# Five more filler matmuls around and within the wide part of an output projection

## The chip, the cores and the metric

The kernel runs on one core of one Trainium2 chip. The metric is the device time of one execution in microseconds; lower is better. Two numbers belong to an execution: the device time, and the span of its instructions on the core, which is 1.4 to 2.0 us shorter. Positions in the traces are counted from the start of the span.

## The reference

The reference mixes two branches with a scalar gate. Branch A is one decode step of attention over long caches; branch B is a gated MLP over a sequence of one. Only A's end matters here.

```python
def reference(A_x, A_k_cache, A_v_cache, A_wq, A_wo, B_x, ..., gate_w):
    g = sigmoid((A_x * gate_w).sum(-1, keepdims=True))
    # A: H = 32 heads, Sk = 16384 keys, Dh = 128, D = 512
    q = (A_x @ A_wq).reshape(...)                     # [1, 32, 1, 128]
    p = softmax(einsum('bhqd,bhkd->bhqk', q, A_k_cache) * Dh ** -0.5)
    o = einsum('bhqk,bhkd->bhqd', p, A_v_cache)
    a = o.reshape(1, 1, 32 * 128) @ A_wo              # output projection, A_wo [4096, 512]
    b = ...                                           # small, done at the start
    return g * a + (1 - g) * b                        # [1, 1, 512]
```

Each cache is 134 MB of bf16. The kernel reads 279.58 MB in all and does little arithmetic for each byte.

## The kernel before

K and V stream through three SBUF buffers. Of the output weights, `wo` has 32 rows for each partition; they are loaded last, in pieces. The projection has two parts. The *wide* part takes rows 0 to 23 in three rounds of eight matmuls with one output row each, in the column groups at 0, 32, 64 and 96 in turn. Their partial sums are copied out by ScalarE (`d_sb`) and folded in with one more product. The *narrow* part takes rows 24 to 31 as they land, two matmuls of 256 columns for each row, in the column groups at 0 and 32.

```python
WO_CUTS = (0, 16, 24, 28, 31, 32)   # pieces of the load, in rows
WIDE, WG = 24, 8

def warm(e, n):              # n fillers: full 128-column matmuls of zeros
    for j in range(n):
        args = (m_ps[0], ident[:, :], zero[:, :])
        ...                  # the first loads its weights, the others don't

def fill(e, m, n=1):         # n fillers of m weight columns (so m output rows), in the column group at 96
    for _ in range(n):
        matmul_again(nc, e, m_ps[0][96:96 + m, :], ident[:, 0:m], zero[:, :], start=True,
                     stop=True, skip_group_check=True)
...
pe.raw(lambda e: warm(e, 2))
t_ok = pe.op(lambda e: e.transpose(oT_ps, o_sb[:, :], ident[:, :]), ...)
...
pe.raw(lambda e: warm(e, 1))
# 4 small matmuls that spread the heads' outputs into o2
...
def pe_wide(e):
    va, pa = (counter(e, n, 0) for n in ("wa", "oa"))
    warm(e, 2)
    with e.Fori(0, WIDE // WG) as t:
        ...                  # 8 matmuls into d_ps, column groups 0, 32, 64, 96 in turn
        registers_first(nc, n, lambda: take(e, wo_s))      # waits for this round's weights
        ins.then_inc(pe.sem, 1)
        fill(e, 1)
        ...
w_ok = act.op(lambda e: e.copy(out=d_sb[:, :], in_=d_ps), wait=[(pe.sem, pe.n)], mark=True)
...
for j, (a, b) in enumerate(zip(WO_CUTS[:-1], WO_CUTS[1:])):
    for k in range(max(a, WIDE), b):                       # narrow part
        y_ok = add(o2[:, k:k + 1], wo[:, k * D:(k + 1) * D],
                   [(ld_o[j], 16)] if k == a else (), k == H - 1)
    if b == 28:
        add(ones_f[:, 0:1], d_sb[:, :], [w_ok])            # folds the wide sums in
# then two copies to res (VectorE, ScalarE) and the store
```

The outputs of `warm` and `fill` are never read.

The softmax here doesn't subtract the row's maximum and nothing guards it: scores larger than these inputs give would overflow.

## Time and profile before

| | before |
|---|---|
| median of the first 3 executions | 651.94 us (651.72 to 652.34) |
| span of the profiled execution | 650.2 us |
| data read | 279.58 MB, 430 GB/s |
| PE / VectorE busy | 65% / 52% of the span |
| load of rows 24 to 27, which the narrow part awaits first, landed | 646.88 us |
| last PE step (20 narrow matmuls) | 1.64 us |

Lines of the profile's page of the kernel before: the span, the busy times, the DMA share in 40 slices (tenths of a slice), and the load queue's share of the 16 DMA engines:

```profile
span 650.2 us, 7735 instructions
PE 423.0 (65%) x2464; PEld 44.4 (7%) x1304; DVE 336.0 (52%) x159; ACT 45.8 (7%) x112; POOL 2.1 (0%) x10
...
DMA  9999989999999999999999989999999999999898
...
q1 hardware_dynamic: 6194, 279.58, 99.6%
```

The loads run from beginning to end; no engine comes near that. Next the end of the chain of waits of the kernel before (start, length, what):

```profile
619.38 27.50 DMA bufs<-in_A_wo_dram
...
646.92 1.64 PE ps_all L716 x20
...
648.58 0.41 DVE res L731
```

The chain names one load of weights, that of rows 24 to 27; then come 1.64 us of narrow matmuls and the copies. A second wait is hidden in that step: the loads of rows 28 to 31 land later, and the last eight narrow matmuls wait for them (their weight loads for 0.47 us, until 647.91). The timeline of PE over the same stretch of the kernel before (start, length, line, what; in brackets the idle time ahead of it). L91 is a filler (the first filler of a `warm` stands under L477), L106 is here a wide round, L716 is the narrow part:

```profile
642.42 0.38 PE L91 MATMUL ps_all<-zero,ident 128*128 128x512 bf16 x1
643.33 0.60 PE L106 MATMUL ps_all<-bufs,o 128*1 x8 [0.54 <-PEq L86]
643.77 0.38 PE L91 MATMUL ps_all<-zero,ident 128*1 128x512 bf16 x1
644.24 0.60 PE L106 MATMUL ps_all<-bufs,o 128*1 x8
...
645.80 0.60 PE L106 MATMUL ps_all<-bufs,o 128*1 x8 [0.73 <-PEq L86]
646.24 0.38 PE L91 MATMUL ps_all<-zero,ident 128*1 128x512 bf16 x1
646.92 0.60 PE L716 MATMUL ps_all<-bufs,o 128*1 128x256 bf16 x8 [0.31 <-DMA bufs<-in_A_wo_dram]
647.36 0.60 PE L716 MATMUL ps_all<-d_sb,const-float32-1.0 128*1 128x256 f32 x4
647.91 0.60 PE L716 MATMUL ps_all<-bufs,o 128*1 128x256 bf16 x8
```

The third wide round waits 0.73 us to be handed its weights, and the narrow part 0.31 us for its load. The fillers lie in between.

Their purpose is the clock. The windows view of the kernel before (stretch; its length; busy time and count for PE, weight loads, VectorE, ScalarE, POOL; then granted PE clock, DMA share, GB/s) shows it at 0.50 after an idle stretch (PE idled from 629.0 to 631.0) and back at 1.00 in the microsecond from 635, and shows it at 1.00 where the narrow part runs (from 646.92 on):

```profile
630.00:631.00 1.00, 0.00 (x0) 0.00 (x0) 0.00 (x0) 0.00 (x0) 0.00 (x0) 1.00 1.04 442
...
632.00:633.00 1.00, 1.00 (x13) 0.31 (x14) 0.00 (x0) 0.00 (x0) 0.00 (x0) 0.50 0.89 377
...
635.00:636.00 1.00, 1.00 (x16) 0.28 (x10) 0.00 (x0) 0.00 (x0) 0.00 (x0) 1.00 1.08 451
...
646.00:647.00 1.00, 0.69 (x11) 0.08 (x4) 0.00 (x0) 0.55 (x1) 0.00 (x0) 1.00 1.02 396
647.00:648.00 1.00, 1.00 (x14) 0.44 (x15) 0.00 (x0) 0.04 (x1) 0.00 (x0) 1.00 0.44 143
```

### The profile page before, as it was taken

The numbers are of one execution on the slowest core, as the hardware profiler recorded it, in microseconds if no ns is written. First come the engines' busy times: TensorE is split into PE (matmuls) and PEld (weight loads), VectorE is DVE, ScalarE is ACT, GpSimd is POOL, SyncE is SP. The second block draws the span as 40 slices with busy tenths as digits, with TensorE's granted clock in tenths as the row PEclk, the third lists the DMA queues.
The fourth block names the chain that finished last, engine by engine and source line by source line (L and its number), as shares of the span: only waits on it lengthen the run. The fifth ranks groups of instructions, "written<-read, shape, count | busy, mean of one in ns | idle before, by whom it ended". The sixth has DMA issues, their size and how long they took to land. (4 is left out here: it accounts for less than half of the span.)

```text
span 650.2 us, 7735 instructions
## 1 busy us (share of the span) xinstructions
PE 423.0 (65%) x2464; PEld 44.4 (7%) x1304; DVE 336.0 (52%) x159; ACT 45.8 (7%) x112; POOL 2.1 (0%) x10
## 2 busy tenths in 40 slices
PE   0547587847387574747857476584747757478767
PEld 0000000000101000010000101000010100001012
DVE  3457848256380845618265370835629075465600
ACT  2200100000001000010100001000010100001011
POOL 1000000000000000000000000000000000000000
PEclk9959788969779696987969798686978968798999
DMA  9999989999999999999999989999999999999898
GB/s 385 462 419 452 452 387 452 452 439 399 452 452 399 439 452 448 391 452 452 407 431 452 452 387 452 452 423 415 452 452 391 448 452 448 391 431 472 390 432 341
DMA packets 6203, 279.60 MB, mean 430 GB/s; under 512 B 695, under 2 KB 826, under 8 KB 1210
## 3 DMA queue, kind: packets, MB, share of 16 engines
q1 hardware_dynamic: 6194, 279.58, 99.6%
q8 instruction: 1, 0.02, 0.0%
q10 hardware_dynamic: 8, 0.00, 0.0%
HBM read 279.58 MB, written 0.00 MB: 430 GB/s over the span
## 5 line engine op out<-in xcount | busy, mean ns | idle before, releaser
L579 DVE TENSOR_TENSOR bufs<-bufs,qb x64 | 281.5, 4419 | 170.8 <-DVEq L86 170.8
L91 PE MATMUL ps_all<-bufs,ident 128*128 x960 | 261.6, 427 | 0.0
L496 PE MATMUL ps_all<-bufs,ident 128*128 x64 | 28.4, 444 | 153.8 <-PEq L86 153.8
L106 PE MATMUL ps_all<-bufs,p_t 128*8 x1024 | 79.2, 385 | 30.7 <-PEq L86 20.1
L564 DVE TENSOR_REDUCE s_sb<-ps_all 128x64 f32<-128x512 f32 x64 | 44.1, 688 | 95.0 <-DVEq L86 95.0
L91 PE MATMUL ps_all<-zero,ident 128*8 128x512 bf16 (+1 forms) x165 | 58.0, 383 | 0.0
L592 ACT ACTIVATE p_t<-s_sb 64x256 f32 (+1 forms) x32 | 13.3, 414 | 433.4 <-ACTq L86 433.0
L496 PEld LDWEIGHTS ps_all<-bufs,ident 128*128 128x128 bf16 x64 | 6.3, 99 | 367.7 <-issue 367.7
L106 PEld LDWEIGHTS ps_all<-bufs,p_t 128*8 x1024 | 17.9, 82 | 163.7 <-issue 163.5
L531 PE MATMUL ps_all<-pick,d_sb 128*128 128x2 f32 x128 | 16.9, 254 | 16.5 <-PEq L86 16.5
L531 PEld LDWEIGHTS ps_all<-pick,d_sb 128*128 128x128 f32 x128 | 15.7, 192 | 34.7 <-issue 34.7
L601 ACT COPY d_sb<-ps_all 128x512 f32<-128x512 f32 x16 | 9.4, 586 | 104.5 <-ACTq L86 104.5
L606 ACT CAST ps_all<-zero 128x512 f32<-128x512 bf16 x15 | 8.8, 589 | 1.7
L666 DVE RECIPROCAL rl<-ps_all 128x32 f32<-128x32 f32 x1 | 0.4, 357 | 11.3 <-PE ps_all L552 11.3
L669 DVE TENSOR_TENSOR o_sb<-ps_all,rl 128x32 bf16<-128x32 f32 x1 | 0.2, 192 | 11.5 <-PE ps_all L531 11.5
L592 ACT ACTIVATION_READ_ACCUMULATOR p_t<-s_sb (+1 forms) x32 | 5.9, 185 | 0.0
L381 DVE TENSOR_TENSOR bufs<-ps_all,ident 128x896 f32<-128x896 f32 x2 | 2.1, 1086 | 7.3 <-PE ps_all L91 7.3
L321 PE MATMUL ps_all<-xgw,const-float32-1.0 1*128 1x3 f32 x2 | 0.6, 360 | 8.0 <-DVE xgw L317 8.0
L106 PE MATMUL ps_all<-bufs,u 128*1 x14 | 2.6, 372 | 3.3 <-ACT ps_all L427 2.5
L91 PE MATMUL ps_all<-bufs,xb 128*128 x12 | 4.1, 467 | 0.0
L345 PE MATMUL ps_all<-bufs,xb 128*128 x4 | 1.9, 485 | 3.1 <-DMA bufs<-in_B_w_in_dram 3.1
L297 PE MATMUL ps_all<-const-bfloat16-1.0,x_row 1*128 1x128 bf16 x4 | 0.6, 302 | 4.8 <-DMA x_row<-in_A_x_dram 4.8
(76 smaller groups left out, 41.2 us busy)
## 6 DMA issues: line engine op xcount, KB each, us to landing
bufs<-in_A_k_cache_dram SPq DMA_DIRECT2D x2, 4096.0 KB, 35.7
bufs<-in_A_v_cache_dram SPq DMA_DIRECT2D x1, 5120.0 KB, 34.0
bufs<-in_A_wq_dram SPq DMA_DIRECT2D x1, 4096.0 KB, 12.3
bufs<-in_A_v_cache_dram SPq DMA_DIRECT2D x1, 2048.0 KB, 38.6
bufs<-in_A_wo_dram SPq DMA_DIRECT2D x1, 2048.0 KB, 24.6
bufs<-in_B_w_in_dram SPq DMA_DIRECT2D x1, 1792.0 KB, 15.5
bufs<-in_A_v_cache_dram SPq DMA_DIRECT2D x1, 1024.0 KB, 40.6
bufs<-in_A_wo_dram SPq DMA_DIRECT2D x1, 1024.0 KB, 26.7
```

The source lines that it names most:

```text
L91: ins = eng.matmul(out, lhsT=lhsT, rhs=rhs, **flags).ins
L106: ins = eng.matmul(bank[0:m, 0:n], lhsT=lhsT, rhs=rhs, **flags).ins
L297: x_ok = pe.op(lambda e, c=c: e.matmul(m_ps[1][:, c * P:(c + 1) * P], lhsT=x_row[0:1, c::DC], rhs=ones_row[0:1, :], start=True, stop=True) ...
L345: if n else matmul_on(nc, e, lambda: e.matmul(args[0], lhsT=args[1], rhs=args[2], **flags), [at, (xa, 0)]))
L381: dve.op(lambda e, h=h, zh=zh: e.tensor_tensor(out=zm[:, 2 * h * ZB:2 * (h + 1) * ZB].rearrange("p (b m k) -> p b m k", b=2, k=FhC), in0=z ...
L496: matmul_on(nc, e, lambda: e.matmul(s3, lhsT=ident[:, :], rhs=k3[:, :, 0:W], start=True, **flags), [(kw, 0)])
L531: ins = e.matmul(o2, lhsT=d_sb[:, r * Dh:(r + 1) * Dh], rhs=pick[:, r * 2:(r + 1) * 2], start=False, stop=False, skip_group_check=True)
L564: return e.tensor_reduce(out=s_sb[:, c * QK:(c + 1) * QK], in_=s_ps[c % 2].rearrange("p (j w) -> p j w", w=W), axis=AX.X, op=ALU.add)
L579: e.tensor_tensor(out=k3, in0=k3, in1=qi, op=ALU.mult).then_inc(mul_s, 1)
L592: e.activation(out=p_t[rows, bass.ds(at, NG * 8)].rearrange("p (t c) -> p t c", c=8)[:, :, 4 * s:4 * s + 4], in_=s_sb[rows, :].rearrange(" ...
L601: return e.copy(out=d_sb[:, :], in_=d_ps)
L606: e.copy(out=d_ps, in_=zero[:, :]).then_inc(drn_s, 1)
```

## The change

The change aims to keep PE busier, and so its clock up, through the end of the kernel; with no filler in the tail, in a run below, the clock stayed at 0.50 from 642.6 us to the end. It adds one filler ahead of the wide rounds, one in each of the three rounds, and one between the last round and the narrow part: five executed matmuls.

```diff
     def pe_wide(e):
         va, pa = (counter(e, n, 0) for n in ("wa", "oa"))
-        warm(e, 2)
+        warm(e, 3)
         with e.Fori(0, WIDE // WG) as t:
             ...
             ins.then_inc(pe.sem, 1)
-            fill(e, 1)
+            fill(e, 1, 2)
             ...
+    pe.raw(lambda e: fill(e, 1))
     for j, (a, b) in enumerate(zip(WO_CUTS[:-1], WO_CUTS[1:])):
         for k in range(max(a, WIDE), b):
             y_ok = add(o2[:, k:k + 1], wo[:, k * D:(k + 1) * D],
```

## The prediction

> **What bounds the kernel now.** The DMA queue. The page's slices show DMA at 9 almost everywhere: 279.58 MB in 650.2 us, packets on 99.6% of the 16 engines' span. PE is busy 65%, DVE 52%. The chain of waits that ended last is, for 27.50 us, one load of output weights (issued at 619.38, landed at 646.88), then 1.64 us of PE (20 narrow matmuls), 0.41 us of DVE copy, and the store.
>
> The tail, from the timeline: fillers at 642.19 and 642.42; wide groups at 643.33, 644.24 and 645.80, each 8 matmuls (0.60 us) and one filler; narrow part at 646.92 (waits for a load), 647.36, and 647.91 (waits for another). Group 3 sits idle 0.73 us before its weights are handed over. So loads pace the tail at three places, and the fillers lie between them.
>
> **What the change does.** It removes and moves nothing. It adds five executed filler matmuls of zeros into an unread region of PSUM: one before the wide loop, one in each of its 3 rounds, one after it. A row of three fillers takes 0.81 us, one 0.38: (0.81 - 0.38)/2 = 0.215 us of array time each, 1.1 us in all. The intent must be the clock: [...] after PE idled from 629.0 to 631.0 the windows view shows 0.50 from 632 to 634 and 1.00 after 635.
>
> **How much is on the critical path.**
> - Before the loop: array free at about 642.64, group 1 at 643.33; 0.215 of 0.69 us is used.
> - Rounds 1 and 2: the period is 0.91 us; group 2 may slip by up to 0.1 us, but group 3 waits for a load until 645.8, which takes that up.
> - Round 3 and after: the filler at 646.24 is followed by two, at about 646.46 and 646.67; the last one's slot ends at about 646.89, the narrow part started at 646.92. They just fit. Slip 0 to 0.1 us, absorbed before 647.91, where the last loads gate again.
>
> Gain: in the profiled run the windows view shows clock 1.00 in every microsecond from 638 to 650, so nothing is to be gained there. If some executions have a cold tail, the narrow part runs at half speed in those, partly hidden behind the loads: estimated from its 1.64 us, 0.3 to 1.6 us. The three timed runs differ by 0.62 us, which leaves room for a few tenths on the median.
>
> **Prediction: 651.85 us, range 651.1 to 652.6.** Faster by over 2%: 0.005; within 2%: 0.99; slower by over 2%: 0.005. If anything, 0.1 us faster.
>
> **What would show it right.** The last chain is still one load of output weights of about 27.5 us, then about 1.64 us of PE; clock 1.00 in the tail; two fillers per wide round and one more before and after.
>
> **What would show it wrong.** The narrow part starting later than its load landed (fillers in the way); a longer last PE step, or narrow matmuls over 300 ns (clock). A change before 642 us cannot follow from this edit.
>
> **What would make it wrong.** A cold tail in most timed runs of before, though not in the profiled one (gain up to 1.6 us); fillers [...] delaying the last matmuls (loss of 0.2 to 0.4 us); chip-to-chip differences in load speed, which would move both kernels.

## The result, and the profile after

| | before | after |
|---|---|---|
| median, first comparison (6 executions each) | 651.78 us (651.63 to 652.34) | 651.65 us (651.61 to 652.38) |
| span of the profiled execution | 650.2 us | 650.3 us |
| third wide round to start of the narrow part | 1.12 us | 1.13 us |
| start of the narrow part to the copies | 1.66 us | 1.65 us |

The ratio is 0.9999, 95% interval 0.9986 to 1.0012: the same. Ratios here and below are the mean time of one kernel's fast executions over that of the other's in the same rounds, so not quite the ratio of the medians quoted.

The page of the kernel after:

```profile
span 650.3 us, 7740 instructions
PE 423.2 (65%) x2469; PEld 44.6 (7%) x1304; DVE 335.9 (52%) x159; ACT 45.8 (7%) x112; POOL 2.1 (0%) x10
```

There are exactly five more PE instructions. The timeline of PE in the kernel after:

```profile
642.57 0.59 PE L91 MATMUL ps_all<-zero,ident 128*128 128x512 bf16 x2
643.47 0.60 PE L106 MATMUL ps_all<-bufs,o 128*1 x8 [0.31 <-PEq L86]
643.91 0.59 PE L91 MATMUL ps_all<-zero,ident 128*1 128x512 bf16 x2
644.38 0.60 PE L106 MATMUL ps_all<-bufs,o 128*1 x8
...
645.95 0.60 PE L106 MATMUL ps_all<-bufs,o 128*1 x8 [0.53 <-PEq L86]
646.38 0.81 PE L91 MATMUL ps_all<-zero,ident 128*1 128x512 bf16 x3
647.08 0.60 PE L716 MATMUL ps_all<-bufs,o 128*1 128x256 bf16 x8
...
648.06 0.60 PE L716 MATMUL ps_all<-bufs,o 128*1 128x256 bf16 x8
```

Everything stands about 0.15 us later than in the trace of before. This shift is there already ahead of the first edited instruction (the small matmul on L677 starts at 642.15 instead of 642.00), so the edit did not cause it. Relative to each other the steps kept their places: the two rounds are still 0.91 us apart, and the narrow part follows the third round by 1.13 us. The idle times became fillers: 0.73 us ahead of the third round is now 0.53, and the 0.31 us ahead of the narrow part are gone. Yet the narrow part starts no sooner. Its wait is still in the trace, on the weight loads, which have no filler ahead of them. First the waits view of before, then that of after (who waited for whom: total us, times, longest):

```profile
PEld ps_all L716 <- DMA bufs<-in_A_wo_dram: 1.5, 2, 1.0
...
PE ps_all L716 <- DMA bufs<-in_A_wo_dram: 0.3, 1, 0.3
```

```profile
PEld ps_all L716 <- DMA bufs<-in_A_wo_dram: 1.5, 2, 1.0
```

The clock is full here too, where the narrow part runs (windows view of the kernel after):

```profile
647.00:648.00 1.00, 1.00 (x13) 0.44 (x12) 0.00 (x0) 0.18 (x1) 0.00 (x0) 1.00 0.52 176
```

The chain of waits of the kernel after looks very different, though nothing moved:

```profile
645.95 0.60 PE ps_all L106 x8
646.55 0.65 PE ps_all L91 x3
647.20 1.51 PE ps_all L716 x20
...
648.73 0.41 DVE res L732
```

It no longer goes back to the load, because PE has no gap left there. A filled gap is not a removed wait: the chain now calls PE the limit, and the experiments below say that it is not.

### The profile page after: what moved, and what is told of

Same layout as the page of the kernel before. It is cut to its first block, busy times and chain, and to the rows that moved or that the text cites. A ratio compares the mean times of both kernels' runs of the same rounds, so it can differ in the third digit from the quotient of the medians.

```text
span 650.3 us, 7740 instructions
## 1 busy us (share of the span) xinstructions
PE 423.2 (65%) x2469; PEld 44.6 (7%) x1304; DVE 335.9 (52%) x159; ACT 45.8 (7%) x112; POOL 2.1 (0%) x10
## 5 line engine op out<-in xcount | busy, mean ns | idle before, releaser
L91 PE MATMUL ps_all<-zero,ident 128*8 128x512 bf16 (+2 forms) x170 | 59.0, 382 | 0.0
L106 PE MATMUL ps_all<-bufs,xb 128*64 x32 | 3.6, 381 | 0.0
```

The source lines that it names most:

```text
L91: ins = eng.matmul(out, lhsT=lhsT, rhs=rhs, **flags).ins
L106: ins = eng.matmul(bank[0:m, 0:n], lhsT=lhsT, rhs=rhs, **flags).ins
```

## The experiments

Theory A: in most executions the clock is full at the end anyway, the loads pace it, and the five fillers lie in slack, so nothing is gained or lost. Rival B: some executions of before end with a cold clock, which the fillers cure, so there is a gain hidden in the spread. A second question is what a filler costs once it no longer fits in slack.

### The changed kernel again (no edit)

> The changed kernel once more, unaltered, with more rounds. Theory A (the clock was already full and the loads gate the tail, so the fillers lie in slack): 651.7 us, within 0.05% of before, clock 1.00 from 638 to 650. Rival B (some executions of before have a cold tail which the fillers cure): before shows more executions of 0.5 us or longer above its lowest than this kernel does, and the mean is 0.1 to 0.3 us lower.

Measured: 651.62 us median of 5 (651.53 to 651.86) against 651.84 for 9 executions of before (651.59 to 652.11); ratio 0.9997, interval 0.9984 to 1.0011. The means differ by 0.17 us in the direction of rival B, and 1 of 9 executions of before against 0 of 5 lies 0.5 us or more above the lowest; neither is clear of noise. The expected clock was wrong, and usefully so: in steps of 0.1 us the windows view has the clock fall at 640.97 us and come back at 644.39. Two of the stretches:

```profile
643.00:644.00 1.00, 1.00 (x3) 0.00 (x0) 0.04 (x1) 0.00 (x0) 0.00 (x0) 0.50 0.98 410
...
646.00:647.00 1.00, 1.00 (x16) 0.17 (x7) 0.00 (x0) 0.40 (x1) 0.00 (x0) 1.00 1.00 388
```

This execution ran at a clock of 0.50 for 3.4 us of its tail and still had the shortest span of the five (650.1 us). A cold stretch that ended before the narrow part cost nothing here, since the loads were waited for in any case (the narrow part started at 646.86).

### No filler at all in the tail

```diff
-    pe.raw(lambda e: warm(e, 2))        # ahead of the transpose
...
-    pe.raw(lambda e: warm(e, 1))        # after it
...
-        warm(e, 2)                      # ahead of the wide rounds
...
-            fill(e, 1)                  # in each wide round
```

> Before without any filler between the last value group and the end: the three fillers around the transpose, the two ahead of the wide part, and those in the wide rounds are all gone. Theory A says the loads still gate; if the clock stays full without them: equal to before within 0.1 us. If the clock does fall to 0.50 there: narrow matmuls about 380 ns instead of 272, last PE step about 0.3 to 1.2 us longer, 652.1 to 652.9 us. Rival B expects the second, and that before itself then sits near the edge.

Measured: 652.75 us median (652.58 to 653.81); ratio to before 1.0013, interval 1.0 to 1.0027; all five spans 651.1 us or more. The trace has the clock fall at 642.6 us and stay at 0.50 to the end, so the second outcome came true. The last steps of its chain of waits:

```profile
620.49 27.48 DMA bufs<-in_A_wo_dram
...
648.01 2.77 PE ps_all L712 x20
```

The load takes 27.48 us, as in the trace of before (27.50), but it was issued 1.11 us later, and the last matmuls ahead of the first removed filler start 1.08 us later too (641.11 instead of 640.03): that part of the length of this execution, the longest of the five, is not the fillers' doing. The 20 matmuls after the load take 2.77 us instead of 1.64. The medians differ by 0.91 us. So fillers as such are worth about 1 us at this place, though only one execution of the five was traced. In before, 33 of the 37 executions counted below have spans under 650.9 us, so its fillers were mostly enough.

### Before without the fillers in the wide rounds

```diff
             ins.then_inc(pe.sem, 1)
-            fill(e, 1)
             e.reg_alu(va, va, 2 * WG * D, ALU.add)
```

> Before without the one filler in each wide round; the five fillers ahead of the wide part stay. Call an execution late when its span is 650.5 us or more, 0.3 above the lowest seen. So far late: before 10 of 23 executions, the changed kernel 1 of 11, before without any tail filler 5 of 5. Rival B (fillers lower the chance of a cold tail, dose by dose): this one late in 3 to 5 of 5, and if the profiled one is late, clock 0.50 during the narrow part and narrow matmuls near 380 ns. Theory A (equal but for chance): late in about as many as before, with clock 1.00 in the narrow part.

Measured: 652.01 us median (651.55 to 653.13), ratio 1.0000; 2 of 5 late by the stated measure, not the 3 to 5 that rival B expected. The profiled one (651.3 us) was late and had a cold narrow part; its bf16 narrow matmuls took 417 ns in the median instead of 272, where 380 was expected. First it, then an execution of before from the same chip and the same rounds:

```profile
646.87 1.02 PE L715 MATMUL ps_all<-bufs,o 128*1 128x256 bf16 x8
...
648.53 1.06 PE L715 MATMUL ps_all<-bufs,o 128*1 128x256 bf16 x8
```

```profile
646.85 0.60 PE L716 MATMUL ps_all<-bufs,o 128*1 128x256 bf16 x8 [0.32 <-DMA bufs<-in_A_wo_dram]
...
647.84 0.60 PE L716 MATMUL ps_all<-bufs,o 128*1 128x256 bf16 x8
```

The narrow parts start within 0.02 us of each other. At clock 0.50 the last of three steps starts 0.69 us later, and the chain of waits gives the whole 2.77 instead of 1.64 us. That is the price of a cold tail: 1.13 us, of a span of 650.

When does it happen? In steps of 0.1 us the clock of this trace changes at 629.5 (down), 636.3 (up), 643.2 (down) and 650.0 (up); in the changed kernel's rerun it changes at 630.7 (down), 634.1 (up), 641.0 (down) and 644.4 (up). All distances are about 3.4 us or twice that: from 629.5 to 650.0 there are six steps of 3.41 us. The changes in both traces fit a grid of that width, which lies elsewhere in each. In this trace it fell at 643.2, before the first wide round (643.27) and so before anything that this kernel lacks. The 3.41 us ahead of the fall held five fillers, one transpose and twelve small matmuls, and no idle time of PE in them exceeded 0.54 us; how busy PE has to be for the clock to stay, these runs do not show. What this kernel lacked came after: the stretch from 643.2 to 646.6 held wide rounds alone, and the clock was still 0.50 at its end. In the rerun of the changed kernel the stretch from 641.0 to 644.4 held four fillers and part of a fifth ahead of the wide rounds, and the clock came back at its end; the first filler of a round started only after that (644.67). So fillers may also work by making the stretch *after* a fall busy; the two traces differ in phase as well, so this is argued and not shown. Whether the one filler per round of before would have been enough in this phase, no trace shows.

Another kept trace bears on the fall itself. The ten-filler run below is the changed kernel up to the end of the wide rounds. Its clock is 0.95 in the mean of 636 to 638 us and 1.00 after, so it came back at about 636.2, and the grid of the two traces above would put a boundary two steps later, at 643.0; against the kernel's own work that is only about 0.17 us earlier than the fall at 643.2 here. The 3.41 us ahead of it hold the same work and one filler more, the one that the change put ahead of the wide rounds (one of the six fillers shows only by its weight load, its matmul record is missing). There the clock stayed at 1.00 to the end. One pair of traces suggests, and does not show, that this filler can prevent the fall in such a phase. That would be rival B's gain.

### Before again, and the changed kernel twice more

> The kernel before once more, as a kernel of its own beside itself, for its trace and for the spread of equal programs. Theory A: ratio 1.000 within 0.05%, times between 651.5 and 652.4 us with a lower cluster near 651.6 and an upper one near 652.0. Rival B (before's upper cluster is executions with a cold tail): if the profiled one is of the upper cluster, its trace shows clock 0.50 at or after 645 us and a last PE step longer than 1.64 us; if of the lower one, clock 1.00 there. Were the upper cluster's trace at clock 1.00 with a later last load instead, B would be wrong and the loads would be the cause.

> Before once more, for another trace and more executions. Rival B: 2 or 3 of these 5 and about 4 of the 9 beside them late (650.5 us or more); if the profiled one is late, its trace shows clock 0.50 in the narrow part. Theory A: late ones have clock 1.00 there and everything, the loads too, shifted.

> The changed kernel once more, for more executions. Rival B: at most 1 of 5 late (650.5 us or more). Theory A: 2 of 5, like before.

> The changed kernel a last time, same expectation: rival B at most 1 of 5 late, theory A 2 of 5. Over the 21 executions of the changed kernel then at hand: rival B at most 4 late, theory A 8 to 10.

Measured, medians of 5 against 9 executions of before beside them (651.92 us in the first, 652.08 in the second):

| | median us | ratio, 95% interval | late (650.5 us or more) |
|---|---|---|---|
| before, first | 651.83 | 0.9999 (0.9986 to 1.0013) | 2 of 5 |
| before, second | 651.68 | 0.9995 (0.9982 to 1.0009) | 0 of 5 |
| changed, first | 651.91 | 0.9997 (0.9983 to 1.0010) | 3 of 5 |
| changed, second | 651.65 | 0.9996 (0.9982 to 1.0010) | 1 of 5 |

In the first look at before (span 650.4 us) the load of rows 24 to 27 landed at 647.13 instead of 646.88, the clock was 1.00 from 637.2 us on, and the last PE step took 1.60 us: its whole tail is 0.23 to 0.28 us later than in the first trace of before, and its loads with it. Before against itself gives 0.9995 in the second look, as far from 1 as the changed kernel gets. Counting every execution whose span was recorded, before was late in 14 of 37 and the changed kernel in 5 of 21. That lies between what the two theories expected (8 to 10, or at most 4, of 21), and shares so different come up by chance about four times in ten (Fisher's exact test, 0.38). A span of 650.9 or more, as a cold narrow part may give (the two traced had 651.3 and 652.4), was seen in 4 of 37 and 1 of 21. The mean device times of these executions are 651.94 and 651.78 us, 0.02% apart; their mean spans are 0.10 us apart. The executions come from two chips. Rival B is neither shown nor excluded; if there is a gain, it is of this size.

One late execution of the changed kernel was profiled, with a span of 650.5 us. Its clock is 1.00 from 636 us to the end, and the third round and the narrow part are both 0.16 us later than in the first trace of the changed kernel:

```profile
646.11 0.60 PE L106 MATMUL ps_all<-bufs,o 128*1 x8 [0.52 <-PEq L86]
...
647.24 0.60 PE L716 MATMUL ps_all<-bufs,o 128*1 128x256 bf16 x8
```

From third round to narrow part it is 1.13 us again. So lateness of 0.3 us need not be the clock in the tail. Nor does a longer cold stretch further up explain it alone: this execution ran at a clock of 0.50 from 629.1 to 635.8 us, but the one traced in the second look ran so from about 629.3 to 636.1 (0.82 in the mean of 628 to 630, 0.98 in that of 636 to 638), with a span of 650.2. Where upstream this shift arises was not followed.

### Ten fillers ahead of the narrow part instead of one

```diff
-    pe.raw(lambda e: fill(e, 1))
+    pe.raw(lambda e: fill(e, 1, 10))
```

> The changed kernel with ten fillers after the wide loop instead of one: 9 x 0.215 = 1.94 us more of array time right before the narrow part. Theory A: the slack there is used up by the change already (last slot of three ends within 0.05 us of the load's landing), so the narrow part starts 1.7 to 1.9 us later, of which the second load wait (0.1 to 0.2 us) gives a little back: 653.2 to 653.6 us. If fillers in their own column group never hold up narrow matmuls: within 0.2 us of before.

Measured: 652.28 us median (652.23 to 652.51), ratio 1.0008, interval 0.9992 to 1.0023. The time lies between the two outcomes: 1.94 us of added array time cost 0.4 to 0.7 us. The trace shows why:

```profile
646.22 1.46 PE L91 MATMUL ps_all<-zero,ident 128*1 128x512 bf16 x6
...
647.31 0.38 PE L716 MATMUL ps_all<-bufs,o 128*1 128x256 bf16 x4
647.52 0.38 PE L91 MATMUL ps_all<-zero,ident 128*1 128x512 bf16 x1
647.52 0.38 PE L716 MATMUL ps_all<-bufs,o 128*1 128x256 bf16 x4
...
648.60 0.38 PE L91 MATMUL ps_all<-zero,ident 128*1 128x512 bf16 x1
649.21 0.36 ACT L732 CAST res<-ps_all 1x256 bf16<-1x256 f32 x1 [2.18 <-PE ps_all L716]
```

Twelve fillers come ahead of the narrow part in the program, but the trace starts only six of them before it; the others run beside it, in their own column group. The narrow part starts 1.53 us after the third round instead of 1.13. The copies then start 1.90 us after the narrow part's start, instead of 1.65. They start 0.23 us after the last filler's end (648.60 + 0.38 = 648.98) and 0.43 us after the modelled end of the last narrow matmul (648.78), though the copies do not wait for a filler; in the trace of before that last gap is 0.07 us. So the fillers cost 0.40 us at the start and 0.25 us at the end of the narrow part, and not their array time. Why six of them hold the start back is not shown.

### Four fillers in each wide round

```diff
-            fill(e, 1, 2)
+            fill(e, 1, 4)
```

> The changed kernel with four fillers per wide round instead of two. Array time of a round: 0.44 + 4 x 0.215 = 1.30 us instead of the period of 0.91. Theory A: groups at 643.5, 644.8 and 646.1 (instead of 643.5, 644.4, 645.95), so the third slips by only 0.1 to 0.2 us, and the five fillers after it delay the narrow part by a further 0.4: end 0.3 to 0.6 us later, 652.0 to 652.3 us. Clock 1.00 as before. If the fillers lie in slack even then: 651.7.

Measured: 652.47 us median (652.0 to 654.01), ratio 1.0014, interval 1.0 to 1.0028. The trace does not show the expected slips. The rounds start at 643.68, 644.59 and 646.15, still 0.91 us apart for the first two, the narrow part 1.15 us after the third (1.13 with two fillers), and the copies 2.77 us after it (2.78). The estimate of 1.30 us for a round added up array time that overlaps: the second round starts at 644.59, ahead of the first round's fourth filler (644.77). This trace's span of 650.5 us comes from further up (the matmul on L677 starts at 642.35 instead of 642.15). The timed executions are nevertheless longer and scattered, with spans from 650.1 to 652.6 us; no trace explains the long ones, and this stays open.

### The last loads taken away, in both kernels

The narrow part reads rows 16 to 23 once more, and rows 24 to 31 are not loaded: a wrong result, with 1 MB less to load and no load to wait for.

```diff
-    for j, (a, b) in enumerate(zip(WO_CUTS[:-1], WO_CUTS[1:])):
+    for j, (a, b) in enumerate(zip(WO_CUTS[:2], WO_CUTS[1:3])):
         sp.op(lambda e, a=a, b=b: e.dma_start(out=wo[:, a * D:b * D], ...
...
-            y_ok = add(o2[:, k:k + 1], wo[:, k * D:(k + 1) * D],
-                       [(ld_o[j], 16)] if k == a else (), k == H - 1)
+            y_ok = add(o2[:, k:k + 1], wo[:, (k - 8) * D:(k - 7) * D], (), k == H - 1)
```

> Before, with the last eight rows of output weights neither loaded nor waited for (the narrow part reads rows 16 to 23 again: wrong result on purpose). If the loads gate the last stage: narrow part starts at about 646.4 instead of 646.92, then the add of the evicted wide sums waits for the scalar engine (about 647.1), end 0.3 to 0.5 us sooner than before: 651.3 to 651.5 us. If the loads don't gate: no change.

> The same cut in the changed kernel (wrong result on purpose). With no load to wait for, the two more fillers between group 3 and the narrow part have nothing to hide behind: narrow part starts 0.2 to 0.4 us later than in the same cut of before, of which part hides behind the scalar engine's copy; end 0.1 to 0.3 us later than that kernel. If fillers in their own column group cost nothing to the narrow matmuls, as the run with ten fillers hints: equal within 0.1 us.

Measured: 651.19 us (651.04 to 652.76) for the cut of before, 651.46 (651.21 to 653.05) for that of the changed kernel; median spans 649.75 and 649.8 us. The ratios (0.9996, interval 0.9981 to 1.0011, and 1.0000, interval 0.9985 to 1.0015) contain one long execution each (652.76 and 653.05 us), so the traces have to decide. The medians lie 0.73 and 0.46 us under that of before. From the third round to the VectorE copy the cut of before takes 2.40 us (645.62 to 648.02), where before takes 2.78 (645.80 to 648.58): the loads did gate the narrow part, by 0.38 us, within the 0.3 to 0.5 expected, and the third round itself stands 0.18 us earlier. The first narrow matmuls start at 646.05 (646.4 was expected). The chain of waits of this cut shows what gates next:

```profile
645.62 0.63 PE ps_all L106 x8
...
646.28 0.59 ACT d_sb L711
...
646.91 1.08 PE ps_all L716 x12
```

It is ScalarE's copy of the wide sums. In the cut of the changed kernel the same stretch takes 2.39 us (645.85 to 648.24), as in that of before. So the expectation of 0.1 to 0.3 us for the changed kernel was wrong, and its alternative right: with no load to hide behind, the two extra fillers still cost nothing. The first eight narrow matmuls (started from 646.28 on) run beside the three fillers there (646.29, 646.50 and 646.72), and all of it hides under ScalarE's copy (646.50, 0.59 us long).

### The fillers as full-array matmuls

```diff
-            fill(e, 1, 2)
+            warm(e, 2)
...
-    pe.raw(lambda e: fill(e, 1))
+    pe.raw(lambda e: warm(e, 1))
```

> The changed kernel with its fillers in and after the wide rounds as full 128-column matmuls (with a weight load) instead of one-column ones. [...] period of the wide rounds 1.0 to 1.2 us instead of 0.91, narrow part 0.1 to 0.3 us late, end 0.1 to 0.4 us later than the changed kernel: 651.8 to 652.1 us. If shape does not matter: 651.6 to 651.7.

Measured: 652.01 us median (651.57 to 652.36), ratio 0.9999, interval 0.9985 to 1.0012; median span 650.2 us. In the trace the first two wide rounds start 1.07 us apart (643.89 and 644.96) instead of 0.91, and the narrow part 1.29 us after the third instead of 1.13. From third round to copies it is 2.83 us instead of 2.78, since the second load wait takes most of it up (0.29 us instead of 0.45). The full-array fillers thus cost about 0.16 us for each round and after the last one, near what was expected, and almost none of it reaches the end.

## Why the prediction was right or wrong

The time was right: 651.85 us predicted, 651.65 measured, inside 651.1 to 652.6, and no effect beyond the noise. Point by point:

- *The loads bound the kernel and pace the tail at three places.* Right. Both traces show the same 1.5 us of weight loads waiting for DMA, and taking the last loads away shortened the stretch after the third round by 0.38 us. The third place, the wait of the third round (0.73 us), stands in the trace but was not taken away.
- *Nothing is to be gained in the profiled run, since the clock is full.* Right for before and after (1.00 from 638 us on in both). For the kernel after it was in part luck: the rerun of the same kernel was at 0.50 from 641.0 to 644.4. What the fillers guard against is real: 1.13 us, in the traces with a cold narrow part. It lies inside the predicted 0.3 to 1.6 us.
- *Group 2 may slip by up to 0.1 us.* It slipped by 0.00; the period stayed 0.91 us.
- *The three fillers after group 3 just fit.* Right in effect: the narrow part follows group 3 by 1.13 us instead of 1.12. But the sum was too strict. Adding array times treats the fillers as a queue in one pipe, while a one-column filler runs beside the narrow matmuls (both start at 647.52 us in the ten-filler run). The expectation for ten fillers was built on that sum and missed by 1 us.
- *The last chain is still one load of about 27.5 us, then about 1.64 us of PE.* Wrong as stated. The chain became all PE (0.60, 0.65 and 1.51 us), because the fillers took the idle time by which the view recognised the load. The wait was unchanged in the waits of the weight loads.
- *If anything, 0.1 us faster.* Not decided. The pooled means differ by 0.16 us in that direction, and the counts of late executions allow chance.
- *Fillers delaying the last matmuls could cost 0.2 to 0.4 us.* It did not arise in the change, whose added fillers inside and after the rounds are one-column like the matmuls beside them (the rounds stayed 0.91 us apart). With full-array fillers each round took about 0.16 us longer (1.07 instead of 0.91), and the loads hid most of it; no run separates the change of shape from the extra weight load of those fillers.

No version here beats both kernels. The one shorter time came from leaving work out.

## What to carry to other kernels

Before adding fillers, look in several executions whether the granted clock is already full where the gated work runs, and whether a load is awaited there; here both held in the first trace of each kernel (1.00, and 1.5 us of waiting weight loads). What more fillers could gain was a bad case of 1.13 us in 650, and 21 executions were too few to see that. The one-column fillers here, in a column group that the narrow matmuls do not use, mostly overlapped with them: nine more, by the estimate above 1.94 us of array time, cost 0.40 us at the start of the narrow part and 0.25 us at its end. Fillers in a group that those matmuls use were not tried. After such a change, read waits from the engine or queue that the fillers do not occupy: the same 1.5 us of waiting weight loads was in both traces, while the chain of waits went from 27.50 us of load to PE alone where the idle time had been filled.
